# Queries of a two-block transformer layer by Strassen's seven products, on a kernel whose MLP already uses them

## The chip, the cores and the metric

The kernel runs on one core of one Trainium2 chip. Its engines run side by side, each through its own list of instructions in order: TensorE (PE, whose weight loads stand apart as PEld), VectorE (DVE), ScalarE (ACT), GpSimd (POOL) and SyncE (SP, which only issues transfers here). The metric is the device time in microseconds, the median of the runs; a lower one is better.

## The reference

2048 rows `x` of width 576 go through an attention block and a gated MLP, each behind a layer norm whose shift, gain and gate come from a vector `c`.

```python
mod = (silu(c) @ w_mod).reshape(1, 6, 1, 576)          # sa, ca, ga, sb, cb, gb
h = layernorm(x) * (1 + ca) + sa
q = (h @ wq)                                           # 2048 x 576 @ 576 x (32 heads * 128)
p = softmax(q_head @ k_head.T * 128**-0.5)             # 16 k/v heads, the last 512 cached keys
x = x + ga * (concat(p @ v_head) @ wo)
h = layernorm(x) * (1 + cb) + sb
x = x + gb * ((silu(h @ w1) * (h @ w3)) @ w2)          # inner width 4608
```

All data is fp32. Every fp32 factor is split into a rounded high part and the rest (`hi`, `lo`, type fp32r), and a product is the sum of three matmuls (hi hi, hi lo, lo hi).

## The kernel before, in words

**Attention** goes over 128 slots, each one head by one block of 512 queries: first the 32 heads for blocks 0 and 1, then again for blocks 2 and 3. The main loop (L1050) has four steps `t` in each slot `i`, one for each 128 queries. In a step PE gets, in this order: `turn(i - 1, t)`, four transposes of the last slot's probabilities; `scores(i, t)`, three 512-column matmuls; `query(i + 1, t)`, 3, 3, 3 and 5 of the 14 matmuls of the next slot's queries; `attend_out(i - 2, t)`, six 288-column matmuls into the one pair of banks `E`. After the fourth step come the 12 matmuls of `values(i - 1)`: in its order high-high, low-high, high-low for each of four key chunks, so that the third matmul is the first that reads the low parts `pt[1]` of the probabilities.

The order is written by hand, and each engine keeps it. DVE gets in a step: the maximum of the scores (L341), the low part of the turned probabilities (`turn_low`, L364, called inside `scores` behind that maximum), and the addition of the head's output onto `acc` (L388); in the fourth step also the low part of the next queries (L85), and after it that of the outputs. ACT gets the high part of the turned probabilities (L358), the exponential (L347), and the high parts of queries and outputs. `run(i, t)` at the end of a step issues whatever `at(...)` has put there: loads, splits and stored work for later.

**Stored work.** The MLP's products are Strassen's: one chunk of 128 inner columns of `w1` beside the same of `w3` is a 2 x 2 block matrix, and two blocks of 512 rows with two halves of the 576 columns are the other. Seven products (`p1` to `p7`) of seven matmuls each replace eight of seven. `make_set` and `make_rows` form, round and store in DRAM the seven combinations of each weight chunk while attention runs; `combine` does the same for the rows `h`. In each, ACT rounds and POOL takes the rest; the store waits on SP for the next step (`store_now`), and each wait of SP holds back the loads queued behind it. The chunks lie in the tag `hs` (seven buffers, which also hold `hT`, the sets of `h` and the modulation weights).

**MLP** (`mlp`, L751): 72 groups of seven products, in between the second matrix (`down`).

**Queries** (`query`, L320; `project`, L282): 14 matmuls for each slot, from raw `wq` columns that POOL and ACT split (`split_in`, L220), and from `hT`, the normed rows of one block turned and split, held on chip for all heads.

PSUM has eight banks: tags `A` and `S` with two buffers (queries and values; scores), `E` with one pair, `T` with two for transposes.

Of the kernel before, what the change touches and what calls it, by code (L numbers as in the profile page):

```python
# [31 lines left out]
PB, QB, RB, HB = 4, 1, 3, 7  # L32

# [5 lines left out]
def tile_block(  # L39
# [28 lines left out]
    def bank(tag, name):  # L68
        return psum.tile([P, 512], F32, tag=tag, name=name)
# [22 lines left out]
    def load_mod(i, rest=None):  # L92
        wm = pool.tile([P, DC, D], F32, tag="hs", name=f"wm{i}", bufs=HB)
        rest = pool.tile([P, D], F32, tag="xn", name="wmr", bufs=ST) if rest is None else rest
# [4 lines left out]
    acc = [const.tile([P, ST, D], F32, name=f"acc{b}") for b in range(NSB)]  # L99

    def load_x(b):
        for t in range(ST):
            lo = b * SB + t * P
            nc.sync.dma_start(acc[b][:, t, :], x[0, lo : lo + P, :])
# [50 lines left out]
    def norm_stats(b, t):  # L155
        if t == 0:
            norms[b] = odd.tile([P, ST, 2], F32, tag="mv", name="mv"), []
        st = odd.tile([P, 2, 6], F32, tag="bst", name="bst")
        for h in range(2):
            nc.vector.bn_stats(st[:, h, :], acc[b][:, t, h * HALF : (h + 1) * HALF])  # L160
        nc.vector.bn_aggr(norms[b][0][:, t, :], st.rearrange("p a b -> p (a b)"))

# [26 lines left out]
    def modulate(hT, m, ps, shift, gain, on_vector=False, tag="hf", bufs=2):  # L189
# [3 lines left out]
        high = hT[m if m < DC else 2 * DC]  # L193
# [6 lines left out]
        if m < DC:  # L200
            eng.tensor_sub(hT[DC + m], hf, high.bitcast(F32))
        else:
            eng.tensor_sub(high[DR:, :], hf[DR:, :], high[DR:, :].bitcast(F32))

    def new_h():

        high = pool.tile([P, DC + 1, SB], F32R, tag="hs", name="hT", bufs=HB)
        low = pool.tile([P, DC, SB], F32R, tag="hs", name="hTl", bufs=HB)
        return [high[:, m, :] for m in range(DC)] + [low[:, m, :] for m in range(DC)] + [high[:, DC, :]]
# [9 lines left out]

    def split_in(raw):  # L220
        wh = pool.tile([P, DC + 1, P], F32R, tag="w", name="wh", bufs=8)
        wl = pool.tile([P, DC + 1, P], F32R, tag="w", name="wl", bufs=8)
        split(wh, wl, raw, nc.gpsimd)
        return wh, wl
# [84 lines left out]

    slots = []
    for half in (0, 2):
        slots += [(half, h, half + b) for b in range(2) for h in range(2)]
        slots += [(half, h, half + b) for h in range(2, HQ) for b in range(2)]
# [3 lines left out]

    def query(i, part):  # L320
        half, h, b = slots[i]
        st = state[i]
        if part == 0:
            st["q"] = bank("A", "pq") if i else E[:, 0, :]
        project(st["q"], wqs[half, h], hT[b], QP[part])
        if part == 3:
            st["qh"] = pool.tile([P, SB], F32R, tag="qh", name="qh", bufs=QB)
            st["ql"] = pool.tile([P, SB], F32R, tag="ql", name="ql", bufs=QB)
            split(st["qh"], st["ql"], st["q"], nc.vector)
# [36 lines left out]
    def values(i):  # L366
# [4 lines left out]
        po = bank("A", "po")  # L371
# [4 lines left out]
        oh = pool.tile([P, SB], F32R, tag="ah", name="oth", bufs=3)  # L376
        ol = pool.tile([P, SB], F32R, tag="al", name="otl", bufs=3)
# [21 lines left out]
    hd, hsets, sets = {}, {}, {}  # L399
    mids = {}  # L400
    hdram = {(pair, k): dram.tile([P, DC + 1, SB], F32, name=f"hd{pair}{k}") for pair in range(PAIRS) for k in ORDER}

    def store_h(b, m, tag, tag_out):

        if m == 0:
            hd[b] = dram.tile([D, SB], F32, name=f"h{b}")
        n = P if m < DC else DR
        ps = turn_rows(b, m, tag)
        hf = pool.tile([P, SB], F32, tag=tag_out, name="hf", bufs=RB if tag_out == "raw" else 2)
        nc.scalar.activation(  # L410
            hf, ps, AF.Identity, bias=vecs["shift", "b"][:, m : m + 1], scale=vecs["gain", "b"][:, m : m + 1]
        )
        nc.sync.dma_start(hd[b][m * P : m * P + n, :], hf[:n])

    def combine_tiles(pair):

        if pair == 0:
            a = pool.tile([P, DC + 1, SB], F32, tag="hs", name="hc", bufs=HB)
            return [a[:, k, :] for k in range(DC + 1)]
        tiles = [pool.tile([P, SB], F32, tag="xn", name="hc", bufs=ST) for _ in range(4)]  # L420
        return tiles + [pool.tile([P, SB], F32, tag="raw", name="hc", bufs=RB)]

    def load_parts(pair, c, tiles):

        for b in range(2):
            src = hd[2 * pair + b]
            for k in range(2):
                dst = tiles[2 * k + b]
                if c < 2:
                    lo = (2 * k + c) * P  # L430
                    nc.sync.dma_start(dst, src[lo : lo + P, :])
                else:
                    lo = DC * P + k * 32
                    for r in range(0, P, 32):
                        nc.sync.dma_start(dst[r : r + 32], src[lo : lo + 32, :])

    def stage(pair, k, c, x):

        def room():
            tag, bufs = ("hf", 2) if pair == 0 else ("raw", RB)  # L440
            return pool.tile([P, SB], F32, tag=tag, name="hst", bufs=bufs)

        hi = room()
        nc.scalar.copy(hi.bitcast(F32R), x)
        if c < 2:
            lo = room()
            nc.gpsimd.tensor_sub(lo.bitcast(F32R), x, hi)
            nc.sync.dma_start(hdram[pair, k][:, 3 + c, :], lo)
        else:
            for r in (32, 96):  # L450
                rows = slice(r, r + 32)
                nc.gpsimd.tensor_sub(hi[rows].bitcast(F32R), x[rows], hi[rows])
        nc.sync.dma_start(hdram[pair, k][:, c, :], hi)

    def combine(pair, c, step, tiles):

        h11, h12, h21, h22, t3 = tiles[:5]
        sub = nc.gpsimd.tensor_sub
        if step == 0:
            sub(t3, h22, h12)  # L460
            stage(pair, "p1", c, h11)
        elif step == 1:
            sub(h12, h12, h11)
            stage(pair, "p2", c, h21)
        elif step == 2:
            sub(h11, h22, h12)
            stage(pair, "p7", c, t3)
        elif step == 3:
            stage(pair, "p5", c, h12)
        elif step == 4:  # L470
            stage(pair, "p6", c, h11)
            sub(h21, h21, h11)
        elif step == 5:
            stage(pair, "p3", c, h22)
        else:
            stage(pair, "p4", c, h21)

    def load_set(pair, k):
        t = pool.tile([P, DC + 1, SB], F32R, tag="hs", name="hset", bufs=HB)
        nc.sync.dma_start(t[:, :, :].bitcast(F32), hdram[pair, k])  # L480
        hsets[pair, k] = t

    wdram = {(f, k): dram.tile([P, DC + 1, P], F32, name=f"wd{f}{k}") for f in range(NF) for k in ORDER}
    works = {}
    staged = [0]

# [10 lines left out]
    def staging(shape, name):  # L497

        staged[0] += 1
        tag, bufs = (("xn", ST), ("w", 8))[staged[0] % 2]  # L500
        return pool.tile(shape, F32R, tag=tag, name=name, bufs=bufs)

    def load_raw(f):

        whole = pool.tile([P, 6, 3, P], F32, tag="hs", name="wraw", bufs=HB)
        cols = slice(f * P, (f + 1) * P)
        for i, w in enumerate((w1, w3)):
# [3 lines left out]
            src = w[DC * P :, cols].rearrange("(k r) n -> r k n", k=2)  # L511
            for r in range(0, P, 32):
                nc.sync.dma_start(whole[r : r + 32, 2 * i : 2 * i + 2, 2, :], src)
        works[f] = whole

    def make_set(f, n):


        a11, a12, a21, a22, s1, s2 = (works[f][:, k] for k in range(6))
        k, x = (("p1", a11), ("p2", a12), ("p4", a22), ("p5", s1), ("p6", s2), ("p7", a21), ("p3", a12))[n]  # L520
        if n == 0:
            nc.gpsimd.tensor_add(s1, a21, a22)
            nc.gpsimd.tensor_sub(s2, s1, a11)
        elif n == 2:
            nc.gpsimd.tensor_sub(a21, a11, a21)
            nc.gpsimd.tensor_sub(a12, a12, s2)
        t = staging([P, DC + 1, P], "wmade")
        nc.scalar.copy(t[:, :3, :], x)
        nc.gpsimd.tensor_sub(t[:, 3:, :], x[:, :2, :], t[:, :2, :].bitcast(F32))  # L529
        nc.gpsimd.tensor_sub(t[DR:, 2, :], x[DR:, 2, :], t[DR:, 2, :].bitcast(F32))  # L530
        store_later(wdram[f, k][:, :, :], t.bitcast(F32))
        if n == 6:
            del works[f]
# [19 lines left out]
    def load_rows(p):  # L553

        whole = pool.tile([P, 7, HALF], F32, tag="hs", name="w2raw", bufs=HB)
# [3 lines left out]
        works["o", p] = whole  # L559

    def keep(x, to, also=None):
# [537 lines left out]
```

## Time and profile before

| | |
|---|---|
| median of 3 runs | 3047.76 us (3047.47 to 3049.01) |
| the profiled execution: its own time | 3051.61 us |
| its span | 3049.5 us |
| attention, 34 to 1804 us: PE busy | 1761.32 of 1770 us |
| there: DVE, ACT, POOL busy | 1266.25, 1055.22, 950.56 us |
| MLP, 1804 to 3049.5 us: PE busy | 1238.41 of 1245.5 us |
| transfers: share, mean rate | 56.3%, 189 GB/s |

The profile is of one execution. A timeline row gives start, duration, engine, line, operation, what it writes and reads, and the count; a square bracket says how long the engine had been idle and what ended that. PE's ends are modelled, so that a 512-column matmul shows about 0.39 us though the next starts after 0.23. In grouped rows the two numbers behind the bar are the busy time and the mean of one in ns, then the idle time before it and what ended most of it.

### The profile page before, as it was taken

The page shows a single profiled execution, that of the slowest core. Times are in us where ns is not written, and L with a number is a line of the kernel's source. Part 1 is how long each engine was busy: PE and PEld are TensorE (multiplying, and loading weights), DVE is VectorE, ACT ScalarE, POOL GpSimd, SP SyncE. Part 2 cuts the span into 40 slices and gives each one's busy share as a digit, 9 for nine tenths or more (in the row PEclk, how much of TensorE's full clock was granted, in tenths as well). Part 3 has the DMA queues.
Part 4 walks back from the last instruction along what each step waited for, and adds up shares of the span by engine and source line. Part 5 has one row for each costly group of instructions (what it writes and reads, how often), then busy time and mean ns, then how long its engine had stood idle before and what let it go on. Part 6 is the DMA issues. An engine that isn't in the chain of part 4 may idle for free.

```text
span 3049.5 us, 47877 instructions
## 1 busy us (share of the span) xinstructions
PE 3021.4 (99%) x16884; PEld 2649.7 (87%) x16884; DVE 1988.0 (65%) x3019; ACT 1451.5 (48%) x3043; POOL 1534.9 (50%) x1587
## 2 busy tenths in 40 slices
PE   7999999999999999999999999999999999999999
PEld 6888888888888888888888888888888888888887
DVE  6777676767776776777777666555555555555556
ACT  4556666666655555556565453333333222222222
POOL 3257887788733620556663003346555455443445
PEclk9999999999999999999999999999999999999999
DMA  5356667666632632465554146667666766666664
GB/s 169 113 168 229 238 204 233 230 217 214 232 100 87 202 125 77 148 214 180 180 193 174 55 146 196 207 217 262 240 231 218 278 224 212 204 202 202 197 200 142
DMA packets 340878, 576.60 MB, mean 189 GB/s; under 512 B 35360, under 2 KB 148000, under 8 KB 338848
## 3 DMA queue, kind: packets, MB, share of 16 engines
q1 hardware_dynamic: 340032, 573.55, 56.3%
q8 instruction: 134, 2.20, 0.3%
q14 instruction: 104, 0.85, 0.1%
q10 hardware_dynamic: 608, 0.00, 0.0%
HBM read 387.58 MB, written 185.83 MB: 188 GB/s over the span
## 4 chain that ended last, share of the span: by engine, by line
PE 94%; DVE 2%; POOL 2%; ACT 1%; DMA 1%; issue 1%; SPq 0%; POOLq 0%; ACTq 0%; DVEq 0%
PE py L609 15%; PE pe L304 12%; PE px L609 11%; PE pq L288 10%; PE pt L357 7%; PE pe L694 7%; PE pf L694 7%; PE po L375 4%; PE po L373 4%; PE po L374 4%; PE pss L337 4%; PE pss L339 4%; PE pss L338 4%; PE pq L296 2%; PE pt L186 0%
## 5 line engine op out<-in xcount | busy, mean ns | idle before, releaser
L347 ACT ACTIVATE p<-pss,nm 128x512 f32<-128x512 f32 x512 | 353.3, 690 | 380.5 <-DVE nm L341 380.2
L609 PE MATMUL py<-hset,wset 128*128 128x512 f32 x2016 | 507.0, 391 | 0.0
L388 DVE SCALAR_TENSOR_TENSOR acc<-pe,r,acc 128x576 f32<-128x576 f32 x512 | 416.9, 814 | 55.0 <-PE pe L304 48.3
L341 DVE TENSOR_REDUCE nm<-pss 128x1 f32<-128x512 f32 x512 | 349.3, 682 | 119.2 <-PE pss L339 119.1
L609 PEld LDWEIGHTS py<-hset,wset 128*128 128x128 f32 x2016 | 362.5, 188 | 59.0
L609 PE MATMUL px<-hset,wset 128*128 128x512 f32 x1512 | 380.2, 391 | 0.0
L304 PEld LDWEIGHTS pe<-o,oth 128*128 128x128 f32 x2048 | 327.0, 188 | 46.6 <-DVE acc L388 4.0
L364 DVE TENSOR_TENSOR ptl<-pt,pth 128x512 fp32r<-128x512 f32 x512 | 349.0, 682 | 13.9 <-ACT pth L358 13.2
L304 PE MATMUL pe<-o,oth 128*128 128x288 f32 x2048 | 356.3, 296 | 0.8 <-DVE acc L388 0.5
L358 ACT CAST pth<-pt 128x512 fp32r<-128x512 f32 x512 | 301.2, 588 | 44.5 <-PE pt L357 40.6
L609 PEld LDWEIGHTS px<-hset,wset 128*128 128x128 f32 x1512 | 275.6, 188 | 49.4
L357 PE MATMUL pt<-ident,p 128*128 128x128 f32 x2048 | 307.8, 273 | 4.6 <-DVE ptl L364 2.6
L85 POOL TENSOR_TENSOR akv<-u,akv 128x512 fp32r<-128x512 f32 x141 | 181.6, 1297 | 233.7 <-ACT akv L84 232.2
L357 PEld LDWEIGHTS pt<-ident,p 128*128 128x128 f32 x2048 | 250.5, 141 | 20.2 <-issue 3.0
L529 POOL TENSOR_TENSOR wmade<-wraw,wmade 128x256 fp32r<-128x256 f32 x252 | 186.1, 739 | 136.0 <-issue 76.0
L337 PE MATMUL pss<-kh,qh 128*128 128x512 f32 x512 | 245.5, 479 | 0.7 <-ACT qh L84 0.7
L85 POOL TENSOR_TENSOR wl<-wraw,wh 128x640 fp32r<-128x640 f32 x64 | 101.0, 1578 | 271.8 <-ACT wh L84 257.9
L85 DVE TENSOR_TENSOR otl<-po,oth 128x512 fp32r<-128x512 f32 x128 | 88.6, 692 | 226.6 <-ACT oth L84 226.6
L304 PE MATMUL pe<-o,otl 128*128 128x288 f32 x1024 | 218.8, 295 | 0.0
L84 ACT CAST oth<-po 128x512 fp32r<-128x512 f32 x128 | 75.1, 586 | 296.3 <-PE po L375 296.3
L339 PE MATMUL pss<-kh,ql 128*128 128x512 f32 x512 | 203.1, 397 | 0.0
L338 PE MATMUL pss<-kl,qh 128*128 128x512 f32 x512 | 202.6, 396 | 0.0
(175 smaller groups left out, 6448.4 us busy)
## 6 DMA issues: line engine op xcount, KB each, us to landing
oset<-od SPq DMA_DIRECT2D x106, 576.0 KB, 4.8
od<-omade SPq DMA_DIRECT2D x133, 288.0 KB, 3.5
kept_o<-o SPq DMA_DIRECT2D x64, 288.0 KB, 3.0
wraw<-in_B_w SPq DMA_DIRECT2D x144, 128.0 KB, 2.9
o<-kept_o SPq DMA_DIRECT2D x32, 576.0 KB, 4.2
wraw<-in_A_wq SPq DMA_DIRECT2D x64, 256.0 KB, 4.0
w2raw<-in_B_w SPq DMA_DIRECT2D x38, 288.0 KB, 3.8
oset<-od SPq DMA_DIRECT2D x35, 288.0 KB, 3.3
```

The lines of the kernel that those rows point to most:

```text
L85: eng.tensor_sub(lo, src, hi.bitcast(F32))
L304: nc.tensor.matmul(E[:, h, :HALF], a[:, rows], b[:, h * HALF : (h + 1) * HALF], start=n == 0, stop=n == 2)
L337: nc.tensor.matmul(pss, st["qh"][:, rows], kh, start=True, stop=False)
L338: nc.tensor.matmul(pss, st["qh"][:, rows], kl, start=False, stop=False)
L339: nc.tensor.matmul(pss, st["ql"][:, rows], kh, start=False, stop=True)
L341: nc.vector.tensor_reduce(nm, pss, axis=AX.X, op=ALU.max, negate=True)
L347: nc.scalar.activation(p, pss, AF.Exp, bias=nm, accum_out=st["l"][:, t : t + 1])
L357: nc.tensor.transpose(ps[:, j, :], p[:, j * P : (j + 1) * P], ident)
L364: nc.vector.tensor_sub(pt[1][:, :, cols], state[i]["t"], pt[0][:, :, cols].bitcast(F32))
L388: nc.vector.scalar_tensor_tensor(a, E[:, :, :HALF], st["r"][:, t : t + 1], a, op0=ALU.mult, op1=ALU.add)
L609: nc.tensor.matmul(ps, w[:, a, :], h[:, b, :], start=start and n == 0, stop=stop and n == 6, skip_group_check=True)
L694: nc.tensor.matmul(ps[:, h, :HALF], a[:, rows], w[:, b, :], start=m == 0, stop=m == 2)
```

## The change

A quad is two heads by two blocks, four slots. Its queries are a product of two block matrices as well: (two blocks of rows) x (two heads). The four first quads keep `query`; the other 28 use seven stored products. `h` of each pair of blocks goes through `combine` into DRAM (kinds 0 and 1), and its seven sets lie on chip for 16 quads; the sets of `wq` are made like those of `w1` and `w3`, 16 of them in all, and loaded for each quad with a lead of four steps. Parts of a product are put into steps by a table; copies and additions on ACT and DVE take the partial sums out of the one bank `Y`.

```python
+    PLAN = {
+        -10: ("p1", 0, 3), -9: ("p1", 3, 7), -8: ("p6", 0, 3), -7: ("p6", 3, 7), -6: ("p5", 0, 2), -5: ("p5", 2, 5),
+        -4: ("p5", 5, 7), -3: ("p3", 0, 2), -2: ("p3", 2, 5), -1: ("p3", 5, 7), 0: ("p2", 0, 3), 1: ("p2", 3, 7),
+        2: ("p7", 0, 3), 3: ("p7", 3, 7), 4: ("p4", 0, 3), 5: ("p4", 3, 7),
+    }
...
+    def strassen(k, name, lo, hi):
+        q = quads[k]
+        if name in ("p1", "p2", "p7") and lo == 0:
+            q["ps"] = bank("Y", "pq")
+        ps = q["ps"]
+        product_steps(qsets[k, name], hsets[k // 16, name], ps, name in ("p1", "p2", "p7"), lo, hi)
+        if hi < 7:
+            return
+        del qsets[k, name]
+        if name == "p1":
+            q["s"] = abuf(4, F32)
+            nc.scalar.copy(q["s"], ps)
+        elif name in ("p6", "p5"):
+            q[name] = pool.tile([P, SB], F32, tag="hf", name="u", bufs=2)
+            nc.scalar.copy(q[name], ps)
+        elif name == "p2":
+            nc.vector.tensor_add(q["s"], ps, q["s"])
+        elif name == "p7":
+            nc.vector.tensor_add(q["p5"], ps, q["p5"])
+        elif name == "p4":
+            nc.vector.tensor_add(q["p6"], ps, q["p6"])
+
+    def queries_ready(i):
+        st = state[i]
+        k, r = divmod(i, 4)
+        src = st.pop("q") if k < PLAIN else quads[k][("ps", "s", "p6", "p5")[r]]
...
+        split(st["qh"], st["ql"], src, nc.vector)
+
+    def project_some(step):
+        i, t = divmod(step, 4)
+        if i + 1 < 4 * PLAIN:
+            query(i + 1, t)
+        for k in range(PLAIN, n // 4):
+            plan = PLAN_FIRST if k == PLAIN else PLAN
+            if step - 16 * k in plan:
+                strassen(k, *plan[step - 16 * k])
...
+    def load_qset(k, name):
+        t = pool.tile([P, DC + 1, P], F32R, tag="w", name="qset", bufs=4)
+        nc.sync.dma_start(t.bitcast(F32), wdram[("q", k % 16), name][:, :, :])
+        qsets[k, name] = t
...
+            project_some(4 * i + t)
             if i < n:
                 scores(i, t)
-            if i + 1 < n:
-                query(i + 1, t)
+            if t == ST - 1 and i + 1 < n:
+                queries_ready(i + 1)
...
+            at(*quarter(16 * k + r - 4), load_qset, k, name)
```

The rest follows from the room that the new sets take:

- `hs` is gone. Seven rooms `h0` to `h6` hold the seven sets of `h`, first of queries, then of the MLP. Raw weight chunks (now 1536 numbers wide, combined in place) lie in these rooms at first, later in the room of the pair of `acc` that is not in use: `x` of blocks 2 and 3 comes in at slot 63, that of blocks 0 and 1 goes to DRAM at slot 66 and is taken back at 118, that of the second pair goes at group 5 of the MLP and is back at 34.
- Norms of blocks 2 and 3 are taken from rows read from DRAM (`look_at`, `look_stats` at slots 34 to 38), and their normed rows again from rows read (`load_rows_of`, `norm_loaded`).
- A planner (`place`) spreads the stored work: 1.35 items a step in steps 65 to 247 (0.75 in 168 to 199), 1.41 in 277 to 469; ten of the 55 chunks of MLP weights are made inside the MLP, with DVE in POOL's place for the rests.
- Staging buffers rotate over `xn` and a new `w2` with four buffers each, in slots 42 to 49 over `w2` alone, later with `raw`.
- PSUM's tag `A` becomes `Y` (queries) and `O` (values) with one buffer each; the outputs' high and low parts have two buffers in place of three.
- The order of the slots in a quad is now (head 0, block 1), (0, 0), (1, 0), (1, 1).

More of the change, by code (lines that the diff above doesn't have):

```diff
@@ L412, in store_h @@
         )
[L413 to L423, printed above, removed]
+        keep_h(kind, b, m, hf)
@@ L425, in load_parts @@
+    def load_parts(kind, c, half, tiles):
+        cols = slice(half * HC, (half + 1) * HC)
         for b in range(2):
-            src = hd[2 * pair + b]
+            src = hd[kind, 2 * (kind % 2) + b]
             for k in range(2):
[L428 to L435, printed above, removed]
@@ L458, in combine @@
+    def combine(kind, c, half, step, tiles):
+        h11, h12, h21, h22, t3 = tiles
         sub = nc.gpsimd.tensor_sub
@@ new lines, in of_q @@
+    def of_q(j):
+        return "w", ("q", j % 16)
+    work = []
+    for p in range(G + 1):
+        work += [("w", f) for f in ((2 * p, 2 * p + 1) if p < G else ())] + [("o", p)]
+    place(
+        "begin", [of_q(4), *of_h(0), of_q(5)],
+        [8 + k * 42 // 56 for k in range(56)], quarter, 5, nc.gpsimd,
+    )
+    steps, due = [], 0.0
+    for step in range(65, 248):
+        due += 0.75 if 168 <= step < 200 else 1.35
+        while due >= 1:
+            steps.append(step)
+            due -= 1
@@ new lines, in tile_block @@
+    assert not asked and not made
+    place("first", items, steps, quarter, 5, nc.gpsimd, 60)
+    late, left = left[-LATE:], left[:-LATE]
+    items, made = [], of_h(2)
+    total = len(left) + len(made)
+    steps = [277 + k * (470 - 277) // (7 * total) for k in range(7 * total)]
+    for k in range(total):
+        items.append(made.pop(0) if made and steps[7 * k] >= 316 and k % 3 == 0 else left.pop(0))
+    place("second", items, steps, quarter, 5, nc.gpsimd, 272)
+    place(
+        "late", late, [84 + k * 147 // (7 * LATE) for k in range(7 * LATE)], product_of, 8, nc.vector, 70
+    )
```

505 lines of the change are left out of this document (310 added, 195 removed).

## The prediction

> **What bounds the kernel now.** I read the page first, then PE's waits over attention, the stretches, and the timeline of one plain slot.
>
> ```profile
> span 3049.5 us, 47877 instructions
> PE 3021.4 (99%) x16884; PEld 2649.7 (87%) x16884; DVE 1988.0 (65%) x3019; ACT 1451.5 (48%) x3043; POOL 1534.9 (50%) x1587
> PE 94%; DVE 2%; POOL 2%; ACT 1%; DMA 1%; issue 1%; SPq 0%; POOLq 0%; ACTq 0%; DVEq 0%
> ```
>
> ```profile
> PE pe L304 <- DVE acc L388: 0.5, 2, 0.3
> PE pq L288 <- DVE nm L341: 0.4, 1, 0.4
> PE po L373 <- ACT pth L358: 0.2, 1, 0.2
> ```
>
> The second fence is all that PE waited for from 200 to 1800 us: 1.1 us in total. So PE's own work is the time, and a matmul that goes is time gained, as long as nothing begins to wait. What keeps PE from waiting is seen in a fourth step of a slot, PE first, then DVE.
>
> ```profile
> 1555.13 0.60 PE L357 MATMUL pt<-ident,p 128*128 128x128 f32 x4
> 1555.49 0.48 PE L337 MATMUL pss<-kh,qh 128*128 128x512 f32 x1
> ...
> 1556.04 0.39 PE L339 MATMUL pss<-kh,ql 128*128 128x512 f32 x1
> 1556.27 0.40 PE L288 MATMUL pq<-hT,wh 128*128 128x512 f32 x1
> ...
> 1557.42 0.69 PE L304 MATMUL pe<-o,oth 128*128 128x288 f32 x4
> ...
> 1558.21 0.39 PE L373 MATMUL po<-pth,vh 128*128 128x512 f32 x1
> 1558.44 0.40 PE L374 MATMUL po<-pth,vl 128*128 128x512 f32 x1
> 1558.67 0.39 PE L375 MATMUL po<-ptl,vh 128*128 128x512 f32 x1
> ...
> 1571.91 0.39 PE L373 MATMUL po<-pth,vh 128*128 128x512 f32 x1
> ```
>
> ```profile
> 1554.78 0.69 DVE L364 TENSOR_TENSOR ptl<-pt,pth 128x512 fp32r<-128x512 f32 x1 [0.24 <-ACT pth L358]
> 1555.38 0.81 DVE L388 SCALAR_TENSOR_TENSOR acc<-pe,r,acc 128x576 f32<-128x576 f32 x1
> 1556.46 0.69 DVE L341 TENSOR_REDUCE nm<-pss 128x1 f32<-128x512 f32 x1 [0.27 <-PE pss L339]
> 1557.07 0.68 DVE L364 TENSOR_TENSOR ptl<-pt,pth 128x512 fp32r<-128x512 f32 x1
> 1558.54 0.69 DVE L85 TENSOR_TENSOR ql<-pq,qh 128x512 fp32r<-128x512 f32 x1 [0.79 <-ACT qh L84]
> ```
>
> Call S the end of the scores, the start of the next matmul: 1556.27. DVE's maximum starts at S + 0.19, the low part behind it ends at 1557.75 = S + 1.48. Its reader, the third matmul of the values (L375), comes at 1558.67, 0.92 us later. Between S and that reader lie five query matmuls (1556.27 to 1557.42, 1.15 us, 0.23 each), six of the output (to 1558.21, 0.79) and two of the values (0.46). The query matmuls are the cover of DVE's pair. From one L373 that opens the values to the next such (1558.21 to 1571.91) a plain slot takes 13.70 us.
>
> **What goes.** 28 quads of 56 query matmuls become 28 of 49: 196 x 0.23 = **45.1 us** less on PE. Stationary and moving tiles keep their sizes, so I keep the 0.23.
>
> **What is late next.** The change puts the query matmuls ahead of the scores in every step, in the four plain quads too. Then S + 0.79 + 0.46 = S + 1.25 is when L375 would run, and its operand is there at S + 1.48. What such a wait costs is in the trace, where DVE was late once:
>
> ```profile
> 102.22 0.68 DVE L341 TENSOR_REDUCE nm<-pss 128x1 f32<-128x512 f32 x1
> 102.82 0.67 DVE L364 TENSOR_TENSOR ptl<-pt,pth 128x512 fp32r<-128x512 f32 x1
> 103.55 0.19 PEld L375 LDWEIGHTS po<-ptl,vh 128*128 128x128 f32 x1 [0.83 <-DVE ptl L364]
> 103.55 0.50 PE L375 MATMUL po<-ptl,vh 128*128 128x512 f32 x1 [0.40 <-DVE ptl L364]
> 103.65 0.19 PEld L373 LDWEIGHTS po<-pth,vh 128*128 128x128 f32 x1
> 103.88 0.40 PE L373 MATMUL po<-pth,vh 128*128 128x512 f32 x1
> ```
>
> The low part ended at 103.49; L375 started 0.06 later, and the matmul behind it 0.33 after that in place of 0.23. So L375 runs at S + 1.54 and the next at S + 1.87, where S + 1.48 was due: **0.39 us in each slot**, whatever the number of query matmuls in the step, since all of them now lie before S. Slots 1 to 127: 127 x 0.39 = **49.5 us** more. Behind the waiting L375 nine matmuls of the values and the next slot's transposes are queued.
>
> The Trainium skill's page "TensorE: Matmul & The Clock Gate" (Architectural detail) says that PE's queue can pull weight loads ahead of matmuls in flight. By that the weights would lie ready and only the bare wait of 0.29 would be paid. The row of 103.55 differs: that load waited with its matmul. It is a rival below.
>
> **The other steps.** The addition onto `acc` follows the low part by 0.60 (1554.78 to 1555.38) and takes 0.81: it ends at S + 0.19 + 0.61 + 0.60 + 0.81 = S + 2.21, with release S + 2.27. The next write of `E` comes at S + 0.79, plus turn 0.36, plus 0.23 for each of k query matmuls, plus scores 0.78: S + 2.39, 2.62 or 2.85 for k = 2, 3, 4. It fits, by 0.12 only where k = 2. That is so for three steps in a quad, 84 in all: I bound a miss between 0 and 0.1 each, 0 to 8 us, and take 3.
>
> ACT's three copies and DVE's three additions in a quad (84 additions at the row below, 58 us) cost nothing: a product's end precedes S by the scores, 0.78, so the addition starts at S - 0.59 and the next instruction can start 0.61 later, at S + 0.02, before the maximum at S + 0.19. The cover is the scores; were DVE still at the last `acc` then (it ends at S - 0.64 where k = 4), each would put up to 0.6 onto the path, 50 us in all, and I keep 0. The norms' statistics are the one real overload: two bn rows are 0.9 us on DVE in 8 second steps and 8 steps in a row, against 0.35 of slack at k = 3 (2.62 - 2.27). I bound that from 0 to 16 x 0.55 = 9 and take 3. The rows below also price the queries' low parts.
>
> ```profile
> L778 DVE TENSOR_TENSOR s<-px,s 128x512 f32<-128x512 f32 x72 | 49.8, 691 | 38.1 <-PE px L609 34.8 <-issue 0.4
> L160 DVE BATCH_NORM_STATS2 bst<-acc 128x6 f32<-128x288 f32 x64 | 25.8, 445 | 4.4 <-DMA acc<-in_A_x 4.4
> L85 DVE TENSOR_TENSOR ql<-pq,qh 128x512 fp32r<-128x512 f32 x127 | 87.9, 692 | 98.6 <-ACT qh L84 98.6
> L85 DVE TENSOR_TENSOR aal<-u,aah 128x512 fp32r<-128x512 f32 x36 | 42.6, 1184 | 24.1 <-ACT aah L84 24.1
> ```
>
> Three of four `ql` now read SBUF twice, as `aal` does: 1184 ns in place of 692. Such a `ql` starts when the exponential and `qh` are done, S + 2.27 in the slot above (1558.54), and ends by S + 3.45; its reader, in the next slot's scores, comes after the output's 0.79, the values' 2.76 and more, past S + 4. That hides it, and 84 x 0.49 = 41 us of DVE are off the path.
>
> **Queues.** Making one weight chunk is 7 x (739 + 459) + 4 x 1016 ns = 12.5 us on POOL, 1.78 an item.
>
> ```profile
> L529 POOL TENSOR_TENSOR wmade<-wraw,wmade 128x256 fp32r<-128x256 f32 x252 | 186.1, 739 | 136.0 <-issue 76.0 <-ACT wmade L528 49.3 <-POOL wmade L530 3.4
> L530 POOL TENSOR_TENSOR wmade<-wraw,wmade 64x128 fp32r<-64x128 f32 x252 | 115.8, 459 | 19.8
> L522 POOL TENSOR_TENSOR wraw<-wraw 128x384 f32<-128x384 f32 x36 | 36.5, 1015 | 1.0
> 300.00:400.00 100.00, 99.59 (x570) 87.25 (x569) 70.83 (x110) 65.25 (x150) 82.78 (x101) 1.00 0.65 223
> 2100.00:2200.00 100.00, 100.00 (x545) 88.23 (x544) 54.79 (x75) 32.74 (x58) 53.73 (x42) 1.00 0.71 248
> SPq L495 <- POOL wmade L530: 322.2, 163, 8.6
> wset<-wd0p SPq DMA_DIRECT2D x14, 320.0 KB, 3.4
> ```
>
> The stretch rows give the busy time of PE, PEld, DVE, ACT and POOL; the first has POOL at 83% with 1.25 items a step. At 1.35 it does 0.18 us more a step, and the raw `wq` splits go; I take the same 83%. SP waits for POOL up to 8.6 us at a store. A set of `wq` is issued four steps ahead, about 13.7 us (a plain slot), and lands in 3.4: 10.3 remain, so PE does not wait, by 1.7 us. Cost 0, bound 0 to 56 (28 quads, 2 us each). The ten chunks moved into the MLP and `x` going out and back lie in the stretch of the second row, where DVE is 55% busy; I cost them nothing, and up to 4 us if DVE is late there. The start of the kernel, where ten more stores of `h` enter SP's queue, gets 0 to 5, taken as 0.
>
> **The sum**, against the profiled 3051.6 us: - 45.1 + 49.5 + 3 + 3 = + 10.4, so 3062.0. That execution lies 3.85 above the median (3051.61 - 3047.76), so the forecast is **3058**.
>
> **Rivals.** (1) *The bare wait*: weights ready, 0.29 a slot, 36.8 us: 12.7 less, 3045. For it: loads elsewhere run one matmul ahead. Against: the row at 103.55. (2) *The saving stays*: DVE's pair comes before L375 after all, no wait: 3058 - 49.5 = 3009, and 3014 with some waits of the same kind in the disturbed slots. It decides if the low part ends before S + 1.2, 0.3 us sooner than in the plain slot, which needs the maximum and the low part to shorten by a fifth or PE's part after S to be longer than I read. For it: all the slack seen today. Against: DVE keeps its order, and both durations are steady. (3) *The sets come late*: POOL, at 83% and more, holds SP's stores, and the sets of `wq` behind them miss their step. It begins to cost where SP is over 10.3 us late; 2 us a quad make 56, 3114. For it: 8.6 us of waits today, when nothing on PE hung on them. Against: a load waits only for the store ahead of it. The Trainium skill's page "SBUF — State Buffer" (Who interferes with whom) adds that a DVE instruction with two SBUF inputs blocks a POOL instruction that reads SBUF, or is blocked by it, for its whole length; the 1184 ns of `aal` agree. By that rule the 84 new ones would hold POOL up to 84 x 0.69 = 58 us more, an estimate. (4) That the change doesn't cut matmuls can't be: seven sevens in place of eight stand in the table.
>
> **How the numbers follow.** Forecast 0.50, (1) 0.10, (2) 0.20, (3) 0.16, a smaller mix 0.04. A measurement here tells apart about 0.2%, 6 us: 3041.7 to 3053.9 counts as the same. The forecast's own range is 3048 to 3072 (the two threes between 0 and 18, the 0.39 by 0.05); I give 0.14 of its 0.50 to the same and 0.36 to slower. Faster: 0.20 + 0.02 = 0.22. Same: 0.14 + 0.08 = 0.22. Slower: 0.36 + 0.16 + 0.04 = 0.56. The range leaves out half of (2) and half of (3): from 3013 to 3092.
>
> **What would show it.** Right: L375 with one wait for L364 in nearly every slot, its first start about S + 1.54, some 37 us or less in PE's waits (a part of the 0.39 is shown as a longer matmul), and plain slots of 13.70 + 0.39. A quad should then last 4 x 13.70 - 1.61 + 1.56 = 54.75 us, as before. Wrong: PE without waits there and a span near 3010; or waits of the products' weight loads for transfers, with SP behind POOL by over 10 us; or waits of L304 for `acc` in most steps, which would say that DVE, not the order at the slot's end, is the bound.

## The result, and the profile after

The changed kernel takes **3141.19 us** (median of 4 runs, 3138.3 to 3144.0) against 3047.84 (4 runs, 3047.47 to 3049.01): a ratio of 1.0306, with a 95% interval of 1.0288 to 1.0323. It is 93 us slower; the forecast was 3058, at most 3092.

The head of the page of after (span; busy time, share and instructions of each engine):

```profile
span 3142.2 us, 49884 instructions
PE 3048.1 (97%) x16688; PEld 2612.0 (83%) x16688; DVE 2121.6 (68%) x3216; ACT 1519.7 (48%) x3299; POOL 1723.2 (55%) x1936
```

The 196 matmuls are gone (16884 to 16688), but PE now idles for 94 us where it idled for 28, and it is busy for 27 us more. To see where, I split each profiled span at two events of the timeline: the start of the first matmul of the values in the second slot, and of that in the last slot.

| us | to the second slot's values | 126 slots | the rest, the MLP |
|---|---|---|---|
| before (span 3049.5) | 74.8 | 1761.1 | 1213.6 |
| after (span 3142.2) | 77.4 | 1803.7 | 1261.1 |
| difference | + 2.6 | + 42.6 | + 47.5 |

Half of the loss lies in the MLP, whose products the change does not touch. Its stretch in before and in after (us of the stretch, busy time of PE, PEld, DVE, ACT and POOL with instructions, granted clock, DMA share, GB/s):

```profile
1835.90:3049.50 1213.60, 1206.52 (x6586) 1064.24 (x6584) 679.86 (x941) 366.50 (x640) 569.64 (x452) 1.00 0.64 215
1881.10:3142.20 1261.10, 1227.44 (x6586) 1073.81 (x6584) 762.15 (x1054) 396.69 (x732) 633.67 (x540) 0.99 0.70 234
```

PE does the same 6586 matmuls there, stands 27 us longer, and is busy 21 us longer. In six places between 2100 and 2415 us the granted clock of after is 0.50, for 34 us in all, in which PE works for 29. At half the clock about 14 of those are lost, an estimate.

Some of the waits of after (engine, line, what it waited for, us in total, times, longest):

```profile
PEld po L517 <- DVE ptl L506: 67.9, 126, 1.0
ACT omade L690 <- DMA hd3p<-hst: 32.6, 11, 6.5
ACT wmade L652 <- DMA hd3p<-hst: 27.4, 10, 7.3
ACT wmade L652 <- POOL acc L648: 17.0, 12, 3.4
PE pe L838 <- DVE acc L832: 9.7, 6, 4.5
PEld pe L385 <- DVE acc L529: 13.3, 41, 1.3
PE pq L748 <- DMA qset<-wq6p: 2.4, 1, 2.4
SPq L613 <- POOL wmade L654: 375.6, 231, 5.0
```

The first row is the forecast wait: L517 is L375 of before, L506 is L364, and it waits in nearly every slot. In before's table 200 to 1800 us had 1.1 us of PE's waits. ACT's rows are new: it waits in all 60 us until a store of a part of `h` (`hst`) has left its buffer, and 17 us for a combination of raw weights on POOL (L648). Here is the fourth step of a plain slot of after, PE with one of its weight loads, then DVE:

```profile
1340.63 0.96 PE L385 MATMUL pe<-o,a 128*128 128x288 f32 x6
1341.42 0.39 PE L515 MATMUL po<-pth,vh 128*128 128x512 f32 x1
...
1342.17 0.19 PEld L517 LDWEIGHTS po<-ptl,vh 128*128 128x128 f32 x1 [0.56 <-DVE ptl L506]
1342.17 0.50 PE L517 MATMUL po<-ptl,vh 128*128 128x512 f32 x1
1342.51 0.40 PE L515 MATMUL po<-pth,vh 128*128 128x512 f32 x1
```

```profile
1340.83 0.69 DVE L483 TENSOR_REDUCE nm<-pss 128x1 f32<-128x512 f32 x1 [0.85 <-PE pss L481]
1341.44 0.68 DVE L506 TENSOR_TENSOR ptl<-pt,pth 128x512 fp32r<-128x512 f32 x1
```

S is 1340.63. L517 starts at S + 1.54, as forecast, and the matmul behind it 0.34 later. The four slots of a plain quad take 12.96, 14.12, 14.12 and 13.63 us from one opening of the values to the next, 54.83 in all (forecast 54.75).

The stretch row that answers to before's of the MLP:

```profile
2100.00:2200.00 100.00, 92.47 (x466) 79.12 (x467) 69.22 (x95) 36.87 (x77) 62.81 (x57) 0.95 0.84 285
```

In this stretch PE does 466 matmuls where it did 545, DVE rises from 55 to 69 us, and the granted clock falls from 1.00 to 0.95.

### The profile page after: what moved, and what is told of

It is laid out like the page before. It is cut to its first block, busy times and chain, and to the rows that moved or that the text cites. A ratio compares the mean times of both kernels' runs of the same rounds, so it can differ in the third digit from the quotient of the medians.

```text
span 3142.2 us, 49884 instructions
## 1 busy us (share of the span) xinstructions
PE 3048.1 (97%) x16688; PEld 2612.0 (83%) x16688; DVE 2121.6 (68%) x3216; ACT 1519.7 (48%) x3299; POOL 1723.2 (55%) x1936
## 5 line engine op out<-in xcount | busy, mean ns | idle before, releaser
L748 PE MATMUL py<-h,wset 128*128 128x512 f32 x2016 | 515.0, 395 | 9.4 <-ACT u L929 8.3
L385 PEld LDWEIGHTS pe<-o,a 128*128 128x128 f32 x3072 | 458.8, 188 | 61.1 <-DVE acc L529 13.3
L385 PE MATMUL pe<-o,a 128*128 128x288 f32 x3072 | 494.9, 297 | 5.6 <-ACT a L86 2.9
L748 PE MATMUL pq<-h,qset 128*128 128x512 f32 x1372 | 429.5, 423 | 8.9 <-DMA qset<-wq6p 2.4
L748 PEld LDWEIGHTS py<-h,wset 128*128 128x128 f32 x2016 | 366.9, 190 | 71.6 <-ACT u L929 9.9
L653 POOL TENSOR_TENSOR wmade<-acc,wmade 128x256 fp32r<-128x256 f32 x308 | 233.4, 758 | 290.4 <-ACT wmade L652 116.9
L748 PE MATMUL px<-h,wset 128*128 128x512 f32 x1512 | 384.6, 394 | 0.1
L506 DVE TENSOR_TENSOR ptl<-pt,pth 128x512 fp32r<-128x512 f32 x512 | 348.4, 680 | 10.1 <-ACT pth L500 9.3
L748 PEld LDWEIGHTS px<-h,wset 128*128 128x128 f32 x1512 | 278.7, 190 | 51.3 <-DVE u L930 0.5
L500 ACT CAST pth<-pt 128x512 fp32r<-128x512 f32 x512 | 300.6, 587 | 13.1 <-PE pt L499 12.9
L748 PEld LDWEIGHTS pq<-h,qset 128*128 128x128 f32 x1372 | 226.5, 191 | 31.8 <-issue 2.6
L517 PE MATMUL po<-ptl,vh 128*128 128x512 f32 x512 | 215.3, 421 | 13.9 <-DVE ptl L506 1.5
```

The costliest lines, as they stand in the source:

```text
L385: nc.tensor.matmul(E[:, h, :HALF], a[:, rows], b[:, h * HALF : (h + 1) * HALF], start=n == 0, stop=n == 2)
L500: nc.scalar.copy(st["pt"][0][:, :, t * P : (t + 1) * P], ps)
L506: nc.vector.tensor_sub(pt[1][:, :, cols], state[i]["t"], pt[0][:, :, cols].bitcast(F32))
L517: nc.tensor.matmul(po, vh[:, j, :], pt[1][:, j, :], start=False, stop=j == KC - 1)
L653: eng.tensor_sub(t[:, 3:, :], x[:, :2, :], t[:, :2, :].bitcast(F32))
L748: nc.tensor.matmul(ps, w[:, a, :], h[:, b, :], start=start and n == 0, stop=n == 6, skip_group_check=True)
```

## The experiments

**Two theories.** The first is the prediction's: the order in the step costs the 0.4 us a slot, and the 47 us of the MLP are a second, separate cost of what was moved there. The rival is one common cause: late sets, full queues and DVE's added work delay everything, and the wait at L517 only shows where it comes out. Each kernel was timed in alternation with before on its chip; before's median lay between 3048.58 and 3049.19 us each time. The ratio is to before.

### The order put back, and the order alone

`order_back` is after with the products' parts behind the scores again:

```
-            project_some(4 * i + t)
             if i < n:
                 scores(i, t)
+            project_some(4 * i + t)
```

> The changed kernel with one thing undone: in each step the scores come again ahead of the query products. Theory (order): the 126 waits of the values' third matmul for the probabilities' low part, some 0.41 us each by slots of 14.12 in place of 13.70, go: 3141 - 52 = 3089; as the slack of 0.9 us also takes up small delays of ACT and DVE, it may be down to 3075. Rival (DVE and the transfers are the bound, the order is a symptom): the waits move to other matmuls, 3130 to 3145.

Measured: 3092.13 us (3088.11 to 3095.66), ratio 1.0140 (1.0125 to 1.0156), 49.1 less than after. The wait has nearly gone:

```profile
PEld po L517 <- DVE ptl L506: 12.0, 27, 1.0
```

The same place of its timeline has product matmuls behind the scores again, and L517 follows its neighbours without a gap (1358.81, then 1359.28, which is twice 0.23, with L516 between):

```profile
1356.86 0.40 PE L481 MATMUL pss<-kh,ql 128*128 128x512 f32 x1
1357.09 1.09 PE L748 MATMUL pq<-h,qset 128*128 128x512 f32 x4
1358.02 0.96 PE L385 MATMUL pe<-o,a 128*128 128x288 f32 x6
1358.81 0.39 PE L515 MATMUL po<-pth,vh 128*128 128x512 f32 x1
1359.28 0.39 PE L517 MATMUL po<-ptl,vh 128*128 128x512 f32 x1
```

A plain quad takes 53.32 us, 1.51 less than after's, and 1.51 less than four plain slots of before (54.83, from the opening of the values at 1517.09 to the fourth one after it, at 1571.91). So with the scores ahead again the seven matmuls that a quad saves are gained nearly whole (7 x 0.23 = 1.61). The values of the second slot come at 73.2 us, so the 2.6 at the start belong to the order too. The MLP is as in after (1261.2): the two costs are separate, and of the 49.1 us 45.6 lie in the 126 slots.

The other direction is the order alone in before. `before_moved` is before with `query` ahead of `scores`:

```
+            if i + 1 < n:
+                query(i + 1, t)
             if i < n:
                 scores(i, t)
-            if i + 1 < n:
-                query(i + 1, t)
```

> The kernel before with one thing done: the query matmuls ahead of the scores in each step, nothing else. Theory (order): 127 slots of 0.39 to 0.41 us, 3048 + 51 = 3099. Rival (such a wait only bites together with the change's extra work): 3048 to 3060.

Measured: 3249.07 us, ratio 1.0651 (1.0635 to 1.0667), far beyond what either theory expected. The edit moved more than the matmuls: in before the split of the queries sits inside `query`, so DVE and ACT got it ahead of the fourth step's maximum and low part. Slots took 15.17 us. `before_moved2` leaves the split behind the scores, as after does:

```
+            if i + 1 < n:
+                query(i + 1, t)
             if i < n:
                 scores(i, t)
-            if i + 1 < n:
-                query(i + 1, t)
+            if t == ST - 1 and i + 1 < n:
+                ready(i + 1)
...
```

> The kernel before with the query matmuls ahead of the scores in each step, and, unlike in the first try, the split of the finished queries left behind the fourth step's scores, as the change has it. Theory (order): 127 slots of 0.41 us, 3048 + 52 = 3100. Rival (the change's loads make the wait): 3048 to 3060.

Measured: 3112.77 us (3112.6 to 3114.2), ratio 1.0207 (1.0192 to 1.0223), 64 above before. Its waits (L378 and L367 are L375 and L364 of before, L360 a transpose):

```profile
PEld po L378 <- DVE ptl L367: 69.9, 124, 1.3
PE pt L360 <- DVE ptl L367: 7.3, 21, 2.6
```

Plain slots are 14.12 us instead of 13.70: 127 x 0.42 = 53 us. The start is 2.6 later, and the second row (2.6 us in before), in slots in which normed rows are turned through the same banks `T`, can make up some 5 of the remaining 8. The MLP is unchanged (1213.6). So the order alone, with nothing of Strassen's products, costs the wait in full, and the rival falls for this part.

### What holds the MLP

`no_late` leaves out the ten weight chunks made inside the MLP (their groups read other chunks of the same size; with them go their raw loads and their work on ACT and DVE); `no_kind3` leaves out the stored parts of `h` of the second pair (its groups read the first pair's):

```
...
-    place(
-        "late", late, [84 + k * 147 // (7 * LATE) for k in range(7 * LATE)], product_of, 8, nc.vector, 70
-    )
```

```
...
-        at(("m", 12 + 3 * k), -1, fill_parts, kind, *w, late_parts)
-        for m in range(7):
-            at(*product_of(7 * (13 + 3 * k) + 2 * m), combine_parts, kind, *w, m)
-            at(*product_of(7 * (13 + 3 * k) + 2 * m + 1), store_now)
```

> The changed kernel without the ten chunks of MLP weights that it makes inside the MLP (left out: the MLP's chunks 30 to 35 of the first weights and 15 to 18 of the second read the stored sets of other chunks). Theory (the MLP's extra 47.5 us are this work's, through the three raw staging buffers that it shares with the parts of h): 3141 - 47 = 3094. Rival (the parts of h alone, now in halves, do it): 3125 to 3141.

> The changed kernel without the parts of h for the MLP's second pair of blocks (left out: combining and storing them; the second half of the MLP reads the first pair's sets), with the ten late chunks kept. Theory (two users share three staging buffers, and ACT waits for a store of the other): the late chunks alone fit, 3096 to 3105. Rival (the late work is by itself too much for ACT, DVE or the buffers there): 3125 to 3141.

Measured: `no_late` 3097.42 us (ratio 1.0160, 1.0143 to 1.0177), 43.8 less than after, its MLP 1214.7. `no_kind3` 3105.13 us (1.0183, 1.0167 to 1.0198), 36.1 less, its MLP 1221.5. Either piece of work alone fits beside the products, with 1 and 8 us over before's 1213.6; the loss needs both. `no_late` still stores every part of `h`, and yet the rows in which ACT waits for `hd3p<-hst` are gone from its waits. What the two pieces share is the tag `raw`, three buffers of staging for what is on its way to DRAM; they share SP's queue too, which these two runs do not tell apart from it.

The chain is seen in one place of after, SP, ACT, DVE, then PE:

```profile
2327.45 0.55 SPq L639 DMA_DIRECT2D acc<-in_B_w  x1
...
2333.19 0.56 SPq L641 DMA_DIRECT2D acc<-in_B_w  x1
...
2334.87 0.38 SPq L613 DMA_DIRECT2D hd3p<-hst  x1
```

```profile
2327.66 0.41 ACT L572 CAST hst<-hc 128x256 fp32r<-128x256 f32 x1 [0.64 <-DMA wd34p<-wmade]
...
2340.08 0.52 ACT L652 CAST wmade<-acc 128x384 fp32r<-128x384 f32 x1 [3.81 <-DMA hd3p<-hst]
...
2341.16 0.58 ACT L920 COPY s<-py 128x512 f32<-128x512 f32 x1
```

```profile
2340.63 0.42 DVE L653 TENSOR_TENSOR wmade<-acc,wmade 128x256 fp32r<-128x256 f32 x1 [3.07 <-ACT wmade L652]
...
2344.22 0.74 DVE L832 TENSOR_TENSOR acc<-pe,acc 128x576 f32<-128x576 f32 x1
```

```profile
2338.81 1.76 PE L748 MATMUL px<-h,wset 128*128 128x512 f32 x7
2345.02 1.81 PE L838 MATMUL pe<-oset,a 128*128 128x288 f32 x6 [4.45 <-DVE acc L832]
2346.63 3.15 PE L748 MATMUL py<-h,wset 128*128 128x512 f32 x7
```

Read from the top: a part rounded at 2327.66 is stored at 2334.87 only; the eight raw loads of the next late chunk take SP from 2327.45 to 2333.75. Its landing frees the buffer for ACT at 2340.08, 5.2 us after its issue. ACT stood at the rounding of a weight for 3.81 us until then; `s<-py`, which the product needs, is behind it. DVE stood behind ACT for 3.07 us at the rest of that weight, and its sums of the products, up to L832, come after that. PE waits 4.45 us for the last of them. Then seven matmuls take 3.15 us instead of 1.76: the stretch from 2340 to 2350 has a granted clock of 0.66.

```profile
2340.00:2350.00 10.00, 5.55 (x19) 4.45 (x18) 6.89 (x10) 3.55 (x8) 5.24 (x6) 0.66 0.74 249
```

A rival for the MLP was DVE: it makes the late chunks' rests in POOL's place, and stands at L653. `late_pool` gives them back to POOL:

```
-        "late", late, [...], product_of, 8, nc.vector, 70
+        "late", late, [...], product_of, 8, nc.gpsimd, 70
```

> The changed kernel with POOL in DVE's place for the rests of the ten late chunks, nothing else. Theory (ACT waits for a free staging buffer, and PE for ACT): little changes, 3130 to 3145. Rival (DVE's wait for ACT's late rounding, 53 us in the trace of that stretch, holds the sums behind it): 3110 to 3120.

Measured: 3141.44 us (3138.93 to 3152.67), ratio 1.0308 (1.0288 to 1.0327): no change from after. So DVE's stand is not the cause. Whether ACT's stand for a buffer is the cause is tested further below, with a fourth buffer.

### What else attention lost

Two candidates, each tried on `order_back`. `ob_lead6` loads the sets of `wq` six steps ahead instead of four:

```
-            at(*quarter(16 * k + r - 4), load_qset, k, name)
+            at(*quarter(16 * k + r - 6), load_qset, k, name)
```

> The changed kernel with the scores ahead again, and the query sets loaded six steps ahead in place of four. Theory (in some seven slots a set lands late, behind raw loads and stores in SP's queue; with the slow clock after it 10 to 15 us): 3077 to 3082. Rival (the sets wait for stores that are late themselves, so a longer lead moves nothing): 3089 to 3095.

`ob_nohold` takes all sets, those of `w2` too, from the first raw block, so that ACT's rounding reads nothing that POOL has combined in place (the sets' values are then others; their size and number are kept):

```
-        k, x = (("p4", a22), ("p1", a11), ("p2", a12), ("p5", a22), ("p7", a21), ("p6", a22), ("p3", a12))[n]
+        k, x = (("p4", a11), ("p1", a11), ("p2", a11), ("p5", a11), ("p7", a11), ("p6", a11), ("p3", a11))[n]
...
-        k, x = (("p1", b11), ("p3", b22), ("p7", y), ("p2", b21), ("p5", b12), ("p6", y), ("p4", b21))[n]
+        k, x = (("p1", b11), ("p3", b11), ("p7", b11), ("p2", b11), ("p5", b11), ("p6", b11), ("p4", b11))[n]
```

> The changed kernel with the scores ahead again, and the stored weight sets rounded from the first raw block for all seven products (left out: the use of the combinations, which POOL still forms; the sets are wrong, their number and size are the same). Then no rounding on ACT waits for POOL's in-place combination. Theory (those waits hold the turned probabilities behind them on ACT, then PE, with a slow clock after it): 3092 - 10 to 20 = 3072 to 3082. Rival (POOL and ACT are simply full, the dependency is a symptom): 3087 to 3097.

Measured: `ob_lead6` 3080.31 us (3076.67 to 3085.22; ratio 1.0105, 1.0088 to 1.0121), 11.8 less than `order_back`. `ob_nohold` 3079.52 us (3075.94 to 3084.63; 1.0099, 1.0084 to 1.0114), 12.6 less. Both are real costs: neither interval meets `order_back`'s. One hold of the second kind in after, ACT, POOL, PE:

```profile
1255.79 0.51 ACT L652 CAST wmade<-acc 128x384 fp32r<-128x384 f32 x1 [2.29 <-POOL acc L648]
1256.21 0.58 ACT L500 CAST pth<-pt 128x512 fp32r<-128x512 f32 x1
```

```profile
1254.76 0.99 POOL L648 TENSOR_TENSOR acc<-acc 128x384 f32<-128x384 f32 x1
```

```profile
1256.84 0.50 PE L515 MATMUL po<-pth,vh 128*128 128x512 f32 x1 [2.10 <-ACT pth L500]
...
1258.15 0.63 PE L515 MATMUL po<-pth,vh 128*128 128x512 f32 x1
1258.58 0.63 PE L516 MATMUL po<-pth,vl 128*128 128x512 f32 x1
```

POOL's two subtractions (L648, L649) stand in one item, behind the rests of earlier items; ACT's rounding of the next item reads the result of the first and waits until it ends at 1255.75, and the high part that the values need (`pth`, L500) is queued behind.

`ob_lead6_spread` is `ob_lead6` with the four combinations spread over items, with at least one item between each and its reader (the sets in the order p4, p1, p5, p2, p7, p6, p3):

```
-        if n == 1:
-            nc.gpsimd.tensor_add(a22, a21, a22)
-            nc.gpsimd.tensor_sub(a21, a11, a21)
...
+        if n == 0:
+            nc.gpsimd.tensor_add(a22, a21, a22)
+        elif n == 2:
+            nc.gpsimd.tensor_sub(a21, a11, a21)
+            nc.gpsimd.tensor_sub(a22, a22, a11)
+        elif n == 3:
+            nc.gpsimd.tensor_sub(a12, a12, a22)
```

> The changed kernel with the scores ahead, the query sets six steps ahead, and the combinations of a weight chunk spread over its seven items, with all ten late chunks as the change has them. Theory (ACT held by POOL's in-place combinations is a cause of its own, worth 12.6 us by the run that took the dependency away): 3080 - 6 to 12 = 3068 to 3074. Rival (the longer lead had already taken those waits, or the order of the items does not help): 3078 to 3083.

Measured: 3073.19 us (3069.81 to 3074.06), ratio 1.0076 (1.0059 to 1.0092): 7 less than `ob_lead6` (the two intervals just overlap), a little over half of the 12.6.

### Versions that mend it

All three have the order put back, the lead of six and the spread combinations. `best_late4` makes four chunks inside the MLP instead of ten, the other six in attention (its stored work goes on to step 493, and `x` comes back at slot 124); `best_ring4` keeps ten and adds a fourth staging buffer, taken in turn by late chunks and parts of `h`; `best_all` does both.

```
-    LATE = 10
+    LATE = 4
...
-    steps = [277 + k * (470 - 277) // (7 * total) for k in range(7 * total)]
+    steps = [277 + k * (494 - 277) // (7 * total) for k in range(7 * total)]
...
-    for pair, away, back_at, then in ((0, (66, 0), (118, 2), (120, 0)), ...
+    for pair, away, back_at, then in ((0, (66, 0), (124, 2), (126, 0)), ...
```

```
+        if spare and staged[0] % 4 == 0:
+            return within(spare[0], 0, shape[1:])
...
-        if kind < 3:
-            t = staging([P, 2, HC], "hst")
-        else:
-            t = pool.tile([P, 2, HC], F32R, tag="raw", name="hst", bufs=RB)
+        t = staging([P, 2, HC], "hst")
...
+        spare.append(pool.tile([P, (DC + 1) * P], F32R, tag="xn", name="spare", bufs=ST))
```

> The changed kernel with the scores ahead, the query sets loaded six steps ahead, the combinations of a weight chunk spread so that a rounding follows its combination by a task, and four late chunks in place of ten (the planner goes on to step 493, x of the first pair comes back at slot 124). Theory (the three causes add up): 3092 - 12 (sets) - 6 to 12 (held ACT) - 30 (late work) = 3038 to 3044. Rival (the six chunks made earlier fill POOL and ACT in attention, so that the waits move there): 3060 to 3075.

> As the one before, but with all ten late chunks left in the MLP and a fourth staging buffer there, which the late chunks and the parts of h take in turn. Theory (ACT waits there for a free buffer): most of the 47 us go, 3092 - 12 - 9 - 30 = 3036 to 3050. Rival (a fourth buffer only shifts the wait, as the stores stand behind loads in SP's queue that wait for PE): 3060 to 3072.

> Both together: four late chunks and the fourth buffer. Theory: 3028 to 3040, below the kernel before. Rival (PE's waits in attention eat it): 3050 to 3065.

| | median us | ratio (95%) | 126 slots | MLP |
|---|---|---|---|---|
| `ob_lead6_spread` | 3073.19 | 1.0076 (1.0059 to 1.0092) | 1739.9 | 1256.7 |
| `best_ring4` | 3049.13 | 0.9999 (0.9990 to 1.0008) | 1736.8 | 1233.3 |
| `best_late4` | 3029.83 | 0.9935 (0.9920 to 0.9951) | 1735.9 | 1217.7 |
| `best_all` | 3029.23 | 0.9938 (0.9925 to 0.9950) | 1733.4 | 1219.2 |

One more buffer, with the work unchanged, takes 24.1 us off the median of `ob_lead6_spread`. The stretches are of the profiled executions, which lie 28.6 us apart, 23.4 of them in the MLP. That is what a shortage of buffers would do. In `best_ring4` ACT still waits (its L691 is after's L690, its L569 after's L572):

```profile
ACT hst L569 <- DMA hd3p<-hst: 13.2, 9, 2.5
ACT omade L691 <- DMA hd3p<-hst: 5.7, 2, 4.5
```

These are 19 us in place of after's 60, so the fourth buffer mends most of it and not all; with four late chunks there is nothing left for it to mend (`best_all` as `best_late4`). `best_late4` and `best_all` beat both kernels, the one before by 0.6%. The head of the page of `best_late4`, and the stretch of its MLP:

```profile
span 3029.6 us, 49798 instructions
PE 2988.8 (99%) x16688; PEld 2609.3 (86%) x16688; DVE 2076.7 (69%) x3145; ACT 1527.0 (50%) x3299; POOL 1763.3 (58%) x2007
```

```profile
1811.90:3029.60 1217.70, 1207.50 (x6585) 1063.82 (x6584) 710.37 (x983) 378.80 (x688) 602.61 (x512) 1.00 0.69 227
```

PE is busy at 99% again, on 16688 matmuls, and the granted clock of the MLP is 1.00. Its 126 slots are 25.2 us shorter than before's, its MLP 4 longer.

## Why the prediction was wrong, point by point

| term | predicted us | measured us | by |
|---|---|---|---|
| matmuls saved | - 45.1 | - 42 (28 x 1.51, an estimate) | plain quads of before and `order_back` |
| low part late in each slot | + 49.5 | + 49.1 | `order_back` |
| sets of `wq` and queues | 0 (to 56) | + 11.8 | `ob_lead6` |
| ACT held behind POOL's combinations | not named | + 12.6 | `ob_nohold` |
| chunks moved into the MLP | 0 (to 4) | + 43.8 | `no_late` |
| `acc`, norms | + 6 | not timed alone | L385's waits for `acc`: 13.3 us in 41 places, 4.0 in 8 before |

The measured terms add up to + 75 of the 93.

**The saving** was there, 1.51 us in a plain quad where 1.61 was forecast. `best_late4`, in which the waits are mostly mended, has its 126 slots 25.2 us shorter than before's.

**What is late next** was right in mechanism, place and size: L517 at S + 1.54, the plain quad to 0.1 us, 0.42 us a slot in `before_moved2` instead of 0.39. That the 49.1 of `order_back` meets the 49.5 so closely is in part luck: some 4 us of it lie ahead of the 126 slots, `order_back` keeps 27 of the waits, and 127 x 0.42 are 53. Rival (1), the bare wait with the weights loaded ahead, did not come: the load of L517 waited with its matmul in 126 slots, though what it loads is `vh`, which lay ready; the late `ptl` is the operand that streams (the 512 columns). The Trainium skill's page "TensorE: Matmul & The Clock Gate" (Architectural detail) has loads pulled ahead of matmuls in flight; these 126 were not. Rival (2) did not come either. The saving and this wait nearly cancel, as forecast: - 42 + 49.1 is + 7, and a change with nothing else in it would have come out near 3055.

**The step that failed** is "The ten chunks moved into the MLP and `x` going out and back lie in the stretch of the second row, where DVE is 55% busy; I cost them nothing, and up to 4 us if DVE is late there". It measured 43.8 us, and 47.5 by the split of the spans; either is enough to carry 3058 out of the range. I looked at the engine that does the work and at its busy share. The late engine was ACT, 37% busy, and what it lacked was a buffer: three for two kinds of work, each of which fits alone. Against `ob_lead6_spread`, a fourth buffer gave back 24.1 us, and four chunks there in place of ten 43.4. That an engine with much free time keeps its order, and that its next instruction serves PE, was worked out for DVE in the prediction; it was not asked of ACT.

**Queues: "Cost 0, bound 0 to 56"** failed too, by 11.8 us. A set was said to have 10.3 us of lead left. The trace has the reason for the longest wait of after: the load stands on SP behind three stores and eight raw loads.

```profile
355.94 7.03 SPq L613 DMA_DIRECT2D wd1p<-wmade  x3
363.02 0.43 SPq L639 DMA_DIRECT2D acc<-in_B_w  x1
...
367.15 0.54 SPq L641 DMA_DIRECT2D acc<-in_B_w  x1
367.79 0.42 SPq L739 DMA_DIRECT2D qset<-wq6p  x1
```

The last of the three stores waited 5.0 us for POOL's rest (the 5.0 of L613 above), the raw loads take SP 4.7 us (363.02 to 367.69), and the set's reader on PE waited 2.38 us. Four steps ahead of that reader the load was due at about 356, so it went some 12 us late, an estimate. That is the mechanism of rival (3), SP held by POOL at the stores, beyond the 10.3 us it asked for, with the raw loads added, which the prediction did not count. PE waited so for six of the 196 sets: ahead of four the trace has both, ahead of one (read at 466.40) raw loads alone, ahead of one (924.77) stores alone. It came at a fifth of the 56 us. SP's longest wait for POOL at these stores fell from 8.6 to 5.0 us, though their sum rose from 322 to 376. POOL did not lose much to the larger `ql`:

```profile
L87 DVE TENSOR_TENSOR ql<-u,qh 128x512 fp32r<-128x512 f32 x56 | 46.1, 824 | 42.9 <-ACT qh L86 42.9
L653 POOL TENSOR_TENSOR wmade<-acc,wmade 128x256 fp32r<-128x256 f32 x308 | 233.4, 758 | 290.4 <-ACT wmade L652 116.9 <-DMA xn<-x 107.3 <-issue 41.6
```

I had priced a `ql` with two SBUF inputs at 1184 ns; it takes 824 in the mean, and the median is 693 (the longest 1636), as for one read from PSUM. The 1184 of `aal` was a mean as well, of 692 to 1290: two SBUF inputs alone do not make the longer time. POOL's rest takes 758 ns instead of 739, 6 us over 308 of them. The 58 us that I had estimated by the Trainium skill's page "SBUF — State Buffer" (Who interferes with whom) did not appear in these rows.

**Not in the prediction:** that ACT can be held by POOL where POOL combines raw weights in place and ACT rounds the result in the next item (12.6 us); and that the clock falls after a wait (last section).

**What stays open.** Of the 93 us some 18 are not shown by an experiment. `acc` and the norms, whose 6 us were not tested, may be among them. `best_late4` still gets only 25.2 of the 42 us in its slots, and the ten late chunks with four buffers still cost about 16 us in the MLP (1233.3 against 1217.7); I have not separated what is left there. `ob_lead6` and `ob_nohold` were measured one by one, so their sum may count something twice. And that the store was late in SP's queue because of the raw loads is read in single places of the trace; no run moved the loads alone, and why the load of `vh` waits with its matmul was not tested.

## What to carry to other kernels

When matmuls are moved, ask what they covered: the distance from the scores to the first reader of DVE's result was the whole of the slack, and it priced the wait to 0.03 us a slot. When work is moved into a stage with idle engines, count its staging buffers and the stores that free them, not only the busy shares: an in-order engine that is 37% busy stops TensorE as soon as its next instruction waits for a buffer, and two pieces of work that each fit may not fit together. Let a combination in place run well ahead of its reader on another engine; one item was too little here.

## What the runs showed of the hardware

A wait of about 2 us on PE can cost more than itself. After the 2.10 us at 1256.84 (PE's fence above) the matmuls went on at half rate: those of 1258.15 and 1258.58 began 0.43 us apart instead of 0.23, and so did the rest up to 1260.71. The granted clock of that stretch was 0.73.

```profile
1255.00:1260.00 5.00, 3.16 (x8) 2.25 (x9) 2.11 (x3) 2.56 (x6) 4.61 (x7) 0.73 0.56 199
```

From 1256.84 to 1260.71 nine matmuls take 3.87 us where nine times 0.23 are 2.07: 1.8 us more (some 0.2 of it L517's own wait for `ptl`), so that the wait cost almost twice what the row of waits says. Not each such wait does so. In `no_late` the one in the same place is as long, and the clock stays at 1.00:

```profile
1254.34 0.50 PE L515 MATMUL po<-pth,vh 128*128 128x512 f32 x1 [2.12 <-ACT pth L500]
1250.00:1260.00 10.00, 7.88 (x42) 6.23 (x41) 5.19 (x9) 4.64 (x11) 8.22 (x13) 1.00 0.55 196
```

From 60 us on after has 13 waits of PE over 1.5 us. With ten of them, from 1.78 us up, the granted clock falls to 0.50 in the wait or within 2 us behind it; with three (1.62, 1.63 and 2.01 us) it does not. The Trainium skill's page "TensorE: Matmul & The Clock Gate" (What's actually happening) has half rate after at least one idle window of about 3.4 us; eight of the ten here were shorter, so the measurement decides; what sets apart the waits that do it is open. The waits of 0.4 us in each slot did not do this: the mean granted clock of `before_moved2` is 0.998, that of after 0.988.
